# Attention and feed-forward in one pass: unread products on PE, mask products moved ahead, one query tile transposed on PE

## The chip, the cores and the metric

The kernel runs on one core of a Trainium2 chip. The metric is the device time of one execution in microseconds (us). The core has five engines that run side by side and wait for each other by semaphores: PE (matrix products; loading its weights is shown apart as PEld), DVE and ACT (elementwise work; ACT has the exponentials and the gelu), POOL (elementwise work on SBUF, and here the queue that issues all loads) and SP (here the queue that issues stores and DMA transposes).

## The reference

Eight batches of eight heads, 576 positions, head width 64. A query sees the keys within 32 positions of it. The result, heads side by side, is the input of a feed-forward layer with 512 inputs and 2048 hidden units.

```python
scores = (q @ k.T) / 8                      # per batch and head
scores = where(|i - j| <= 32, scores, -1e9)
attn   = softmax(scores)
x      = (attn @ v)  ->  4608 tokens x 512
h      = x @ w_in                           # 512 x 2048
g      = h * sigmoid(1.702 * h)
out    = g @ w_out                          # 2048 x 512
```

## The kernel before

All 8 x 576 positions are treated as one line of 4608 tokens. A **unit** u is 128 of them (36 units), a **window** w is two units, and a **tile** i is 512 tokens of queries or keys (9 tiles). Everything is in bf16, sums are in f32 in PSUM. The order of all instructions is written out by hand; nothing is moved by a scheduler. Each engine works through its own list in that order, so an instruction that waits holds up all that stand behind it on its engine.

The steps of one unit:

- `load_heads` and `load_v` (POOL queue) load queries and keys of a tile, and V of a unit (`ve`). `odd_v` copies V shifted by 64 tokens into `vo`.
- `keys_T` and `queries_T` turn a tile: PE transposes against the identity into a PSUM bank `tp`, and a copy (line 99) brings it into the rings `kT` and `qT`, for one pair of heads at a time. A faster form first lets DVE pair up the heads (`pair_heads`, into `kc` and `qc`), so that four transposes of 128 x 128 do a pair instead of eight. From tile 3 on, queries are not turned on PE: `queries_X` issues one DMA transpose of the whole tile on the SP queue. `queries_wrap` copies the first columns of the query ring behind its end, on DVE, when a tile lands at the ring's start (tiles 0, 3 and 6).
- `scores` (line 221): 32 or 64 small products into two banks of kind "a", then the exponential on ACT into `p` (line 227).
- `band` (lines 242 and 247): DVE multiplies `p` by a 0/1 mask, two products of 128 x 512 for a unit. The last unit, 35, has another layout and takes four products of 128 x 256, on line 247.
- `values` (line 258): PE multiplies `p` by `ve` and `vo`; a column of ones gives the softmax sum. `norm` (lines 269 and 270): DVE takes the reciprocal and scales into `x`.
- `x_T`: `x` is turned, in the opening on PE and with a copy, later by a DMA transpose on the SP queue.
- `layer1` (line 297): eight products of 128 x 256 and one gelu on ACT (line 299) make one of eight groups for two units. `layer2` (line 308): sixteen products of 128 x 512 in four quarters; then DVE copies the bank `o_ps` to `o_sb` (line 312) and SP stores it.

PSUM has eight banks, handed out by kind: two "h" (layer 1, and layer 2 of odd units), one "o" (layer 2 of even units), one "t" (transposes), four "a" (scores, values, some transposes).

Two layers lie between attention and output: window w runs attention for units 2w and 2w+1, layer 1 for window w-1 and layer 2 for window w-2. `head` is the opening: it prepares the masks, loads, turns tiles 0, 1 and 2, and runs the attention of units 0 to 6 with the first layers in between. In batch 0 the tokens 512 to 575 end a batch in the middle of a unit, and so queries and keys of these 64 tokens are loaded and turned apart (`load_edge`, `edge_T`). `window` runs windows 4 to 19; window 4 has an order of its own. At its end `feed` prepares what the next window needs: the shifted V, the paired heads, and in odd windows the query transpose of a tile.

Three places in it matter for the change. In window 4, the four key blocks of tile 3 alternate with groups of layer 1, and `queries_X(3)` is issued ahead of them (lines 504 to 513). In windows 5 to 14, which have two key blocks each, DVE's list has a key copy, the o_sb copy, the first mask products, the other key copy, and the second mask products. In the opening, the edge of the keys is turned and copied between the scores of units 0 and 1 and their mask products (lines 364 to 369), and its load stands behind three loads of V (lines 331 to 335).

Of the kernel before, what the change touches and what calls it, by code (L numbers as in the profile page):

```python
# [15 lines left out]
F32 = mybir.dt.float32  # L16
BF16 = mybir.dt.bfloat16
# [4 lines left out]
JT = 4  # L22
# [5 lines left out]
class _Kernel:  # L28
# [35 lines left out]
    def setup(self):  # L64
        nc, cst = self.nc, self.cst
        self.ident = cst.tile([128, 128], BF16, name="ident")
        self.mask = cst.tile([128, 4, SQ], BF16, name="mask")
        self.w_in_sb = cst.tile([128, self.NK, self.DFF], BF16, name="w_in_sb")
        self.w_out_sb = cst.tile([128, self.NFF, self.DM], BF16, name="w_out_sb")
        self.kT = cst.tile([128, 4, RING + 64], BF16, name="kT")  # L70
        self.qT = cst.tile([128, 4 * JT, RP + 16], BF16, name="qT")
        self.k_first = cst.tile([128, 4, 64], BF16, name="k_first")
        self.q_first = cst.tile([128, 4 * JT, 8], BF16, name="q_first")
        self.ve = [cst.tile([128, self.H, 66], BF16, name=f"ve{i}") for i in range(NV)]
        self.vo = [cst.tile([128, self.H, 66], BF16, name=f"vo{i}") for i in range(NV)]
        self.v_first = cst.tile([64, self.H, 66], BF16, name="v_first")
        make_identity(nc, self.ident)
        for i in range(NV):
            nc.vector.memset(self.ve[i][:, :, self.D:], 1.0)
# [63 lines left out]

    def heads_T(self, c, i, hp, kind):

        tp = self.bank(kind, [128, JT, 128], BF16, "tp")
        for j in range(JT):
            for t in range(2):
                self.nc.tensor.transpose(tp[64 * t:64 * t + 64, j, :],  # L149
                                         self.stage[c, i][:, 2 * hp + t, j * self.D:(j + 1) * self.D], self.ident)  # L150
        return tp

    def keys_T(self, i, hp, kind="t", eng=None):

        if ("k", i, "c") in self.stage:
            tp = self.bank(kind, [128, JT, 128], BF16, "tp")
            for j in range(JT):
                self.nc.tensor.transpose(tp[:, j, :], self.stage["k", i, "c"][:, hp, j], self.ident)  # L158
        else:
            tp = self.heads_T("k", i, hp, kind)  # L160
        at = (512 * i) % RING

        def put(dst, n):
            self.cast(eng or self.nc.vector, dst.rearrange("r (p j) -> r p j", j=JT),
                      tp[:, :, :n // JT].rearrange("r j p -> r p j"))

        put(self.kT[:, hp, at:at + 512], 512)
        if at == 0 and i:
            put(self.kT[:, hp, RING:], 64)
# [131 lines left out]
    def layer2(self, u, quarter, kind="o"):  # L301
# [8 lines left out]
        if quarter == 3:  # L310
# [7 lines left out]
            else:  # L318
                n = self.N - row
                nc.sync.dma_start(self.out[row:row + n, :], o_sb[:n])  # L320
                nc.sync.dma_start(self.out[0:128 - n, :], o_sb[n:])


    def head(self):

        nc, dve, act, pool = self.nc, self.nc.vector, self.nc.scalar, self.nc.gpsimd
        self.setup()
        for h in (0, 4):
            for c in "kq":
                self.load_heads(0, c, (h, h + 4))  # L330
        for m in range(3):
            self.load_v(m)
        self.setup_mask()
        for c in "kq":
            self.load_edge(c)
        self.load_v(3)
        self.load_v(4, 0)
        self.load_w_in(0)
        self.load_w_in(1)
# [16 lines left out]
        for c in "kq":  # L356
            self.load_heads(2, c)
        kinds = "htho"
        for half in (0, 2):
            for hp in (half, half + 1):  # L360
                self.keys_T(0, hp, kinds[hp], dve)
            for hp in (half, half + 1):
                self.queries_T(0, hp, kinds[hp ^ 2], act)
        self.scores(0)
        self.scores(1)
        self.edge_T("k", "h", dve)
        self.edge_T("q", "h", act)
        self.band(0)
        self.band(1)
        self.scores(2)  # L370
        self.values(0, "hh")
        self.norm(0)
# [25 lines left out]
        l2 = [(lambda c=c, u=u: self.layer2(u, c, "hhot"[u])) for c in range(4) for u in range(4)]  # L398
# [25 lines left out]
        run(1)  # L424
        self.x_T(4, "a")
        run(1)
        self.x_T(5, "a")
        self.load_v(8)
        self.load_v(9)
        self.load_v(10)  # L430
# [27 lines left out]
    def window(self, w):  # L458
# [9 lines left out]
        def run(lst, n=1):  # L468
            for _ in range(min(n, len(lst))):
                lst.pop(0)()  # L470
# [9 lines left out]
        if w == 4:  # L480
# [23 lines left out]
            for c in "qk":  # L504
                for hp in range(4):
                    self.pair_heads(c, 3, hp, dve)
                if c == "q":
                    self.queries_X(3)
            run(l1, 3)
            for _ in range(3):  # L510
                run(kt)
                run(l1)
            run(kt)
            self.feed(w)
            return
        loads()
# [2 lines left out]
            if w > 5:  # L519
                self.scores(b)  # L520
        run(l2, 2)
        run(kt)
        run(l2)
        if w == 5:
            self.scores(b)
        run(l2)
        if att:
            self.band(a)
        run(kt)
        run(l2)  # L530
        if att:
            self.band(b)
        run(l2)
        if att:
            self.values(a)
            self.values(b)
            self.norm(a)
            self.x_T(a)
            self.norm(b)
            self.x_T(b)  # L540
        run(l2, 2)
        run(l1, 4)
        self.feed(w)
# [73 lines left out]
```

## Time and profile before

| what | value |
|---|---|
| median of 3 runs | 341.6 us (340.18 to 343.05) |
| the profiled execution | 341.15 us |
| its span, from the first to the last instruction | 339.5 us |
| what lies around the span | 1.65 us |
| mean granted clock of PE | 0.99 |
| PE busy | 304.7 us, 90% of the span |
| ACT, DVE and POOL busy | 174.1, 146.6 and 73.0 us |

A row of the timeline gives the start, the duration, the engine, the line and the operation with its tiles, how many were merged into the row (x16), and in brackets how long the engine was idle before it and what ended the wait. L297 is line 297 of the kernel. A row that merges several instructions begins with the first and covers them all. In the view of stretches each engine has its busy time and number of instructions, then come the clock, a DMA share and GB/s. PE's products overlap in a pipeline, so their rows overlap too, and the distance from one start to the next tells the pace. A few records of products are missing, which leaves small gaps such as 0.16 us "issue" in front of a row with x7 instead of x8.

### The profile page before, as it was taken

Reading aid. Unit: us, or ns where it says so; the run is one execution under the profiler, and the core shown is the slowest. Engines: PE = TensorE matmul, PEld = TensorE weight load, DVE = VectorE, ACT = ScalarE, POOL = GpSimd, SP = SyncE. Lnnn points to the kernel's source line nnn. Section 1 sums busy time; section 2 is a strip of 40 time slices with the busy share of each in tenths; the row PEclk is TensorE's granted clock in tenths of the full one; section 3 lists DMA queues with packets and bytes.
Section 4 is the critical chain, followed back from the end, with each engine's and each line's share of the span. In section 5 each row is a group of like instructions: output and inputs, shape, how many; then the busy total and the mean of one; then the engine's idle time right before and its main releaser. Section 6 shows DMA issues by size and latency. Waiting matters only on the chain.

```text
span 339.5 us, 8719 instructions
## 1 busy us (share of the span) xinstructions
PE 304.7 (90%) x3748; PEld 207.4 (61%) x3784; DVE 146.6 (43%) x433; ACT 174.1 (51%) x263; POOL 73.0 (22%) x107
## 2 busy tenths in 40 slices
PE   1789999899919979999999999999999999989994
PEld 1558754656605748575757576766666675748571
DVE  1362057458507262727182818181816153442101
ACT  1555554482603727474737383838382837474150
POOL 8993464306003120322040202020200000000000
PEclk9999999999978999999999999999999999999999
DMA  7999999948984999399959989671953040302011
GB/s 89 171 199 193 186 193 190 185 84 100 149 87 58 144 118 119 55 157 128 99 65 155 147 74 80 110 87 41 93 95 75 22 86 14 90 20 75 28 35 62
DMA packets 94429, 35.29 MB, mean 104 GB/s; under 512 B 67256, under 2 KB 89784, under 8 KB 94392
## 3 DMA queue, kind: packets, MB, share of 16 engines
q0 software_dynamic: 61760, 18.49, 60.5%
q1 hardware_dynamic: 32632, 16.26, 29.3%
q8 instruction: 29, 0.48, 0.6%
q14 instruction: 8, 0.07, 0.1%
HBM read 36.96 MB, written 9.44 MB: 137 GB/s over the span
## 4 chain that ended last, share of the span: by engine, by line
PE 74%; DVE 12%; DMA 7%; issue 3%; POOL 2%; ACT 1%; POOLq 0%; ACTq 0%
PE h_ps L297 37%; PE o_ps L308 30%; DMA qT<-qc 5%; DVE p L242 4%; DVE o_sb L312 3%; PE sc L221 3%; PE pv L258 3%; DMA edge<-in_k_dram 2%; DVE kT L99 2%; PE tp L149 1%; DVE x L270 1%; PE tp L158 1%; POOL ve L133 1%; DVE p L247 1%; ACT p L227 1%
## 5 line engine op out<-in xcount | busy, mean ns | idle before, releaser
L299 ACT ACTIVATE g<-h_ps 128x512 bf16<-128x512 f32 x144 | 86.0, 597 | 123.8 <-PE h_ps L297 123.8
L297 PE MATMUL h_ps<-xT,w_in_sb 128*128 128x256 bf16 x1152 | 133.4, 275 | 2.8 <-DVE xT L99 2.1
L308 PE MATMUL o_ps<-w_out_sb,g 128*128 128x512 bf16 x540 | 129.0, 381 | 6.8 <-issue 6.3
L297 PEld LDWEIGHTS <-w_in_sb 128*128 128x128 bf16 x1152 | 112.4, 98 | 21.5 <-issue 2.5
L308 PEld LDWEIGHTS <-g 128*128 128x128 bf16 x576 | 52.5, 98 | 57.5 <-issue 2.9
L133 POOL DMA_DIRECT2D ve<-in_v_dram x40 | 33.8, 851 | 161.3 <-PE pv L258 98.1
L99 DVE COPY kT<-tp 128x512 bf16<-128x512 bf16 (+2 forms) x45 | 26.0, 596 | 97.8 <-PE tp L158 65.8
L312 DVE COPY o_sb<-o_ps 128x512 f32<-128x512 f32 x36 | 24.9, 691 | 68.6 <-PE o_ps L308 67.0
L227 ACT ACTIVATE p<-sc 128x512 bf16<-128x512 f32 x70 | 36.4, 602 | 12.8 <-PE sc L221 12.7
L270 DVE TENSOR_TENSOR x<-pv,rec 128x256 bf16<-128x256 f32 x72 | 30.6, 425 | 2.5
L242 DVE TENSOR_TENSOR p<-p,mask 128x512 bf16<-128x512 bf16 x70 | 27.1, 428 | 1.5 <-ACT p L227 1.1
L221 PE MATMUL sc<-qT,kT 64*64 64x64 bf16 x1152 | 15.3, 200 | 7.6 <-DVE qT L189 7.1
L258 PEld LDWEIGHTS <-p 128*64 128x64 bf16 x576 | 13.7, 115 | 13.8 <-DVE p L242 8.5
L299 ACT ACT_TABLE_LOAD x16 | 20.5, 1283 | 0.3
L258 PE MATMUL pv<-ve,p 128*64 128x65 bf16 x288 | 18.7, 203 | 1.9 <-DVE p L242 0.4
L221 PEld LDWEIGHTS <-kT 64*64 64x64 bf16 x1152 | 12.7, 113 | 12.4 <-issue 12.0
L227 ACT ACT_TABLE_LOAD x15 | 19.2, 1283 | 0.3
L258 PE MATMUL pv<-vo,p 128*64 128x65 bf16 x288 | 18.6, 203 | 0.7 <-DVE p L247 0.6
L99 ACT COPY qT<-tp 128x512 bf16<-128x512 bf16 (+1 forms) x13 | 7.2, 571 | 15.8 <-PE tp L149 15.5
L269 DVE RECIPROCAL rec<-pv 128x4 f32<-128x4 f32 x72 | 12.5, 174 | 6.2 <-PE pv L258 6.2
L127 POOL DMA_DIRECT2D qs<-in_q_dram x17 | 12.3, 731 | 3.4 <-DMA w_out_sb<-in_moe_w_out_dram 1.8
L127 POOL DMA_DIRECT2D ks<-in_k_dram x17 | 12.2, 723 | 2.0 <-DMA qs<-in_q_dram 1.2
(42 smaller groups left out, 100.4 us busy)
## 6 DMA issues: line engine op xcount, KB each, us to landing
out_dram<-o_sb SPq DMA_DIRECT2D x70, 128.0 KB
ve<-in_v_dram POOLq DMA_DIRECT2D x32, 128.0 KB, 7.7
w_in_sb<-in_moe_w_in_dram POOLq DMA_DIRECT2D x4, 512.0 KB, 7.6
w_out_sb<-in_moe_w_out_dram POOLq DMA_DIRECT2D x4, 512.0 KB, 10.6
ks<-in_k_dram POOLq DMA_DIRECT2D x4, 256.0 KB, 8.4
qs<-in_q_dram POOLq DMA_DIRECT2D x4, 256.0 KB, 12.0
ks<-in_k_dram POOLq DMA_DIRECT2D x2, 448.0 KB, 10.7
qs<-in_q_dram POOLq DMA_DIRECT2D x2, 448.0 KB, 14.1
```

Source lines behind the costliest of these rows:

```text
L99: (eng.copy if eng is self.nc.scalar else eng.tensor_copy)(out, in_)
L127: self.nc.gpsimd.dma_start(self.stage[key][off // JT:(off + m) // JT, lo:hi, :], src[b, lo:hi, s:s + m, :].rearrange("h (p j) d -> p h (j ...
L133: self.nc.gpsimd.dma_start(self.ve[m % NV][off:off + n, :, :self.D], self.v[b, :, s:s + n, :].rearrange("h s d -> s h d"))
L221: nc.tensor.matmul(sc[eo][lo:lo + 64, 2 * hp + blk, :], self.kT[r, hp, at:at + 64], self.qT[r, JT * hp:JT * hp + JT, q0:q0 + 16], start=(n ...
L227: nc.scalar.activation(p[:, eo], sc[eo], AF.Exp, scale=self.scale)
L242: self.nc.vector.tensor_mul(pv, pv, msk.to_broadcast([128, 4, 2, SQ]))
L258: nc.tensor.matmul(acc[half][blk * 64:blk * 64 + 64, hh, :], p[:, h % 2, h // 2 * 2 + blk, :], vt[:, h, :D + 1], start=(hh == 0), stop=(hh ...
L270: nc.vector.tensor_mul(x[:, hs, :], acc[half][:, :, :D], rec[:, hs, :].to_broadcast([128, 4, D]))
L297: nc.tensor.matmul(hps[:, i, :], self.w_in_sb[:, kr, ff * 128:(ff + 1) * 128], self.xT[t][:, kr, :], start=(i == 0 and kr == 0), stop=(i = ...
L299: nc.scalar.activation(self.g[t][:, 2 * d:2 * d + 2, :], hps, AF.Gelu_apprx_sigmoid)
L308: nc.tensor.matmul(o_ps, self.g[t][:, ff, s * 128:(s + 1) * 128], self.w_out_sb[:, ff, :], start=(ff == 0), stop=(ff == self.NFF - 1))
L312: nc.vector.tensor_copy(o_sb, o_ps)
```

## The change

Five edits, all in the order of the work or in who does it; the result stays the same.

1. `keep_busy(n)` issues n products of a cleared operand (128 x 128 by 128 x 256) into a bank of kind "a" that nobody reads. In the opening there are 24 ahead of the first key transposes, then 10, 6, 4 and 1 between the transposes of keys and queries: 45 in all. DVE clears the operand `idle` first of all.
2. The edge queries and keys are loaded ahead of V and of the mask's preparation; and the mask products of units 0 and 1 stand ahead of the edge's transposes and copies.
3. The copy of unit 5's `x` goes from DVE to ACT.
4. In window 4 the queries of tile 3 are turned on PE from the paired heads (`heads_T` now has that form too), one pair behind each pair of keys, with the copy on ACT. The DMA transpose of tile 3 is gone; those of later tiles stay.
5. In the later windows both units' mask products follow the first key copy directly. The second key block goes behind the values and norms. In window 5 the second scores go ahead of the first key block.

```diff
+        self.idle = cst.tile([128, 256], BF16, name="idle")
+        nc.vector.memset(self.idle, 0.0)
...
     def heads_T(self, c, i, hp, kind):
         tp = self.bank(kind, [128, JT, 128], BF16, "tp")
         for j in range(JT):
+            if (c, i, "c") in self.stage:
+                self.nc.tensor.transpose(tp[:, j, :], self.stage[c, i, "c"][:, hp, j], self.ident)
+                continue
             for t in range(2):
...
     def keys_T(self, i, hp, kind="t", eng=None):
-        if ("k", i, "c") in self.stage:
-            tp = self.bank(kind, [128, JT, 128], BF16, "tp")
-            for j in range(JT):
-                self.nc.tensor.transpose(tp[:, j, :], self.stage["k", i, "c"][:, hp, j], self.ident)
-        else:
-            tp = self.heads_T("k", i, hp, kind)
+        tp = self.heads_T("k", i, hp, kind)
...
+    def keep_busy(self, n):
+        junk = self.bank("a", [128, 256], F32, "junk")
+        for _ in range(n):
+            self.nc.tensor.matmul(junk, self.idle[:, 0:128], self.idle, start=True, stop=True)
...
     def head(self):
...
-        for m in range(3):
-            self.load_v(m)
-        self.setup_mask()
         for c in "kq":
             self.load_edge(c)
-        self.load_v(3)
+        self.setup_mask()
+        for m in range(4):
+            self.load_v(m)
...
+        self.keep_busy(24)
         for half in (0, 2):
             for hp in (half, half + 1):
                 self.keys_T(0, hp, kinds[hp], dve)
+            self.keep_busy(4 if half else 10)
             for hp in (half, half + 1):
                 self.queries_T(0, hp, kinds[hp ^ 2], act)
+            self.keep_busy(1 if half else 6)
         self.scores(0)
         self.scores(1)
+        self.band(0)
+        self.band(1)
         self.edge_T("k", "h", dve)
         self.edge_T("q", "h", act)
-        self.band(0)
-        self.band(1)
...
-        self.x_T(5, "a")
+        self.x_T(5, "a", act)
...
     def window(self, w):
...
                     self.pair_heads(c, 3, hp, dve)
-                if c == "q":
-                    self.queries_X(3)
-            run(l1, 3)
-            for _ in range(3):
+            run(l1, 2)
+            for hp in range(4):
                 run(kt)
+                self.queries_T(3, hp, "a", nc.scalar)
                 run(l1)
-            run(kt)
             self.feed(w)
             return
...
         run(l2, 2)
-        run(kt)
-        run(l2)
         if w == 5:
             self.scores(b)
+        run(kt)
         run(l2)
         if att:
             self.band(a)
-        run(kt)
-        run(l2)
-        if att:
             self.band(b)
         run(l2)
+        run(l2, 2)
         if att:
             self.values(a)
...
             self.x_T(b)
+        run(kt)
         run(l2, 2)
```

In the opening, DVE's list changes behind the key copies of tile 0 (the copies are line 99 before and line 101 after; `pv` is the values' bank). Before:

```order
L99 COPY kT<-tp 128x512 x4
L99 COPY kT<-tp 128x4x64
L242 TENSOR_TENSOR p<-p,mask 128x512 x4
L269 RECIPROCAL rec<-pv_366 128x4
L270 TENSOR_TENSOR x<-pv_366,rec 128x256
```

and after the change:

```order
L101 COPY kT<-tp 128x512 x4
L242 TENSOR_TENSOR p<-p,mask 128x512 x4
L101 COPY kT<-tp 128x4x64
L269 RECIPROCAL rec<-pv_418 128x4
L270 TENSOR_TENSOR x<-pv_418,rec 128x256
```

The four mask products of units 0 and 1 have moved ahead of the edge copy (128x4x64).

In window 6, DVE's list from its first key copy to the copy behind the norms is before:

```order
L99 COPY kT_70<-tp_2004 128x512
L312 COPY o_sb_2018<-o_ps_1995 128x512
L242 TENSOR_TENSOR p_1955<-p_1955,mask_67 128x512 x2
L99 COPY kT_70<-tp_2024 128x512
L242 TENSOR_TENSOR p_1992<-p_1992,mask_67 128x512 x2
L269 RECIPROCAL rec_2078<-pv0_2041 128x4
...
L312 COPY o_sb_2100<-o_ps_2030 128x512
```

and after the change:

```order
L101 COPY kT_70<-tp_2079 128x512
L242 TENSOR_TENSOR p_2030<-p_2030,mask_67 128x512 x2
L242 TENSOR_TENSOR p_2067<-p_2067,mask_67 128x512 x2
L312 COPY o_sb_2097<-o_ps_2070 128x512
...
L270 TENSOR_TENSOR x_2154<-pv1_2129,rec_2155 128x256
L101 COPY kT_70<-tp_2161 128x512
L312 COPY o_sb_2175<-o_ps_2101 128x512
```

Both pairs of mask products now stand ahead of the first o_sb copy, and the second key copy stands between the last norm and the second o_sb copy.

In window 4, PE's list around the last key block of tile 3 and the scores of unit 10 (`h_ps` is layer 1's bank, `kc` and `qc` the paired heads; each row of weights and product comes four or eight times) is before:

```order
L297 MATMUL h_ps_1610<-xT_1106,w_in_sb_68 128x256
L158 LDWEIGHTS kc_1534
L158 MATMUL tp_1620<-ident_66,kc_1534 128x128
...
L221 LDWEIGHTS kT_70
L221 MATMUL sc0_1637<-qT_71,kT_70 64x64
```

and after the change:

```order
L152 LDWEIGHTS kc_1585
L152 MATMUL tp_1679<-ident_66,kc_1585 128x128
...
L152 LDWEIGHTS qc_1580
L152 MATMUL tp_1686<-ident_66,qc_1580 128x128
...
L297 LDWEIGHTS w_in_sb_68
L297 MATMUL h_ps_1692<-xT_1158,w_in_sb_68 128x256
...
L221 MATMUL sc0_1712<-qT_71,kT_70 64x64
```

Four transposes of queries follow each four of keys, and a group of layer 1 now stands between the last transposes and the scores.

## The prediction

> **What bounds the kernel now.** I read the page's totals first.
>
> ```profile
> span 339.5 us, 8719 instructions
> PE 304.7 (90%) x3748; PEld 207.4 (61%) x3784; DVE 146.6 (43%) x433; ACT 174.1 (51%) x263; POOL 73.0 (22%) x107
> ```
>
> PE sets the end. Its work can hardly shrink, so what can be won is time in which PE stands still, or runs slowly: 339.5 - 304.7 = 34.8 us idle. To see where, I cut the span at the scores that open each window, with the view of stretches (the first row is window 5, then 6, 7, 9 and 15; the column after the stretch is its length, then PE busy).
>
> ```profile
> 90.61:115.92 25.31, 17.61 (x199) 11.54 (x200) 11.13 (x35) 9.18 (x14) 4.62 (x6) 0.87 1.05 83
> 115.92:133.82 17.90, 15.76 (x199) 10.86 (x200) 7.66 (x22) 9.41 (x14) 1.76 (x2) 1.00 1.74 139
> 133.82:150.29 16.47, 15.98 (x199) 11.04 (x200) 8.64 (x26) 9.41 (x14) 5.06 (x7) 1.00 0.91 90
> 166.76:183.36 16.60, 15.98 (x200) 11.04 (x201) 8.86 (x28) 9.41 (x14) 3.50 (x4) 1.00 0.80 84
> 265.82:281.47 15.65, 15.33 (x191) 10.51 (x193) 5.99 (x18) 9.41 (x14) 0.00 (x0) 1.00 0.24 52
> ```
>
> Windows 5 to 14 issue the same work, yet window 5 takes 9 us longer, at a mean clock of 0.87. The timeline says why:
>
> ```profile
> 84.98 9.61 SPq L184 DMA_TRANSPOSE qT<-qc  x1
> 101.31 0.20 DVE L189 COPY qT<-qT 128x128 bf16<-128x128 bf16 x1 [8.11 <-DMA qT<-qc]
> 101.56 0.59 PE L221 MATMUL sc<-qT,kT 64*64 64x64 bf16 x28 [7.09 <-DVE qT L189]
> ```
>
> The DMA transpose of tile 3's queries starts at 84.98 and is only done 16.3 us later. DVE's wrap copy waits for it, the scores of unit 11 wait for the copy, and PE idles 7.1 us.
>
> **Tile 3 queries on PE: -9.1.** Added are 16 transposes on PE and 4 copies on ACT; one DMA transpose and its packets go. The host is a loop like this one:
>
> ```profile
> 88.97 0.40 PE L158 MATMUL tp<-ident,kc 128*128 128x128 bf16 x4
> 89.20 1.04 PE L297 MATMUL h_ps<-xT,w_in_sb 128*128 128x256 bf16 x8
> 89.41 0.82 DVE L99 COPY kT<-tp 128x512 bf16<-128x512 bf16 x2 [0.49 <-PE tp L158]
> 90.28 0.23 PEld L158 LDWEIGHTS <-kc 128*128 128x128 bf16 x4 [0.32 <-DVE kT L99]
> L99 ACT COPY qT<-tp 128x512 bf16<-128x512 bf16 (+1 forms) x13 | 7.2, 571 | 15.8 <-PE tp L149 15.5
> L299 ACT ACTIVATE g<-h_ps 128x512 bf16<-128x512 f32 x144 | 86.0, 597 | 123.8 <-PE h_ps L297 123.8
> ```
>
> Rounds start every 1.31 us (88.97, 90.28), because the one bank of kind "t" is free only when DVE has copied it (89.41 + 0.82). PE issues 0.23 + 0.87 in a round, so 0.2 is spare, and four more transposes (0.23) just fill it. ACT's round is one gelu and one copy, 0.60 + 0.57, under 1.31. The last round gains a group of layer 1 that stood earlier before, so in all I count +0.1. The wrap copy then stands behind 6 DVE copies (about 2 us after the last key copy), while PE has a layer-1 group, scores and 8 products of layer 2 to issue (about 3 us): hidden, and if that cover failed, some tenths. A window with keys and no stall is window 15 plus two key blocks, 15.65 + 2 x 0.22 = 16.1. So 25.3 - 16.1 = 9.2, less 0.1. That includes about 1.3 of slow clock behind the gap. Bounds: 7.1 (the idle row alone) and 9.5.
>
> **Mask products straight behind the exps: -4.0.** Window 8 shows the order that the change rewrites (the last two rows are window 15):
>
> ```profile
> 152.31 2.07 ACT L227 ACTIVATE p<-sc 128x512 bf16<-128x512 f32 x4
> 154.85 0.69 DVE L312 COPY o_sb<-o_ps 128x512 f32<-128x512 f32 x1 [1.03 <-PE o_ps L308]
> 156.12 0.69 DVE L99 COPY kT<-tp 128x512 bf16<-128x512 bf16 x1
> 156.72 0.75 DVE L242 TENSOR_TENSOR p<-p,mask 128x512 bf16<-128x512 bf16 x2
> 156.69 0.22 PE L258 MATMUL pv<-ve,p 128*64 128x65 bf16 x1
> 158.10 1.67 PE L308 MATMUL o_ps<-w_out_sb,g 128*128 128x512 bf16 x7 [0.16 <-issue]
> 271.78 0.22 PE L258 MATMUL pv<-ve,p 128*64 128x65 bf16 x1
> 272.81 1.67 PE L308 MATMUL o_ps<-w_out_sb,g 128*128 128x512 bf16 x7 [0.16 <-issue]
> ```
>
> Between the exps, done at 154.38, and the second pair of mask products, done at 157.47, DVE copies an o_ps and a key tile; PE reached the values at 156.69, and their block lasts 158.10 - 156.69 = 1.41. In window 15, without key copies, it lasts 1.03, and in window 6, where PE came late, 0.87 (124.30 to 125.17). So six windows lose 0.54, the two of 16.60 another 0.13 each, windows 15 and 16 lose 0.16: 6 x 0.54 + 2 x 0.67 + 0.3 = 4.9. Behind the change both pairs (0.75 each) end near 155.2 and nothing waits. What is late next: the second key copy now stands between the norms and the copy of o_ps, whose bank the second layer-1 group needs. By the rows' durations the norms end 2.6 after the values begin, the key copy at 3.3, the o_sb copy at 4.0, and PE wants the bank at 3.9: about 0.1 in 9 windows, 0.9 in all. Bounds: 1.5 and 4.9.
>
> **Window 6 and the last values: -2.0.** Two more rows, and the exps and products of unit 35:
>
> ```profile
> 122.92 1.46 PE L308 MATMUL o_ps<-w_out_sb,g 128*128 128x512 bf16 x6 [1.82 <-issue]
> 300.11 2.44 ACT L229 ACTIVATE p<-sc 128x512 bf16<-128x512 f32 x2
> 302.73 2.08 DVE L247 TENSOR_TENSOR p<-p,mask 128x256 bf16<-128x256 bf16 x4
> ```
>
> The 1.82 in window 6 has no semaphore behind it, and falls inside a group of products. Nothing in the change removes it; a stall tied to the instruction stream's place may move or go. I take half, -0.9 (bounds 0 and -1.8). For unit 35 the last of four products (0.52 each) ends at 304.8; behind the second exp (302.55) its two remaining products would end at 303.6: -1.1 (bounds -0.5 and -1.2).
>
> **Unit 5's copy on ACT: -0.8.**
>
> ```profile
> 59.99 0.41 DVE L99 COPY xT<-tp 128x512 bf16<-128x512 bf16 x1
> 60.45 0.81 PE L297 MATMUL h_ps<-xT,w_in_sb 128*128 128x256 bf16 x6 [1.57 <-DVE xT L99]
> ```
>
> Layer 1 waits for the last copy of its input, which stands behind an o_sb copy on DVE. ACT is idle then and takes about 0.59; PE starts near 59.6, when unit 4's copy on DVE is done too. Bounds 0.4 and 0.9.
>
> **The opening: -2.2.** Here three edits meet: 45 unread products (24, 10, 6, 4, 1), edges ahead of V, and products ahead of the edge copy.
>
> ```profile
> 4.59 2.67 POOL L133 DMA_DIRECT2D ve<-in_v_dram  x3
> 15.00:20.00 5.00, 4.36 (x110) 3.19 (x110) 4.17 (x13) 3.78 (x8) 4.72 (x8) 1.00 1.33 201
> 5.63 1.07 PE L149 MATMUL tp<-ident,ks 128*64 128x128 bf16 x16 [5.63 <-DMA ks<-in_k_dram]
> 11.71 1.06 PE L149 MATMUL tp<-ident,qs 128*64 128x128 bf16 x16 [0.36 <-DVE kT L99]
> 13.58 0.69 POOL L140 COPY vo<-ve 64x528 bf16<-64x528 bf16 x1
> 13.88 2.06 ACT L227 ACTIVATE p<-sc 128x512 bf16<-128x512 f32 x4 [0.41 <-PE sc L221]
> 15.69 0.29 DVE L99 COPY kT<-tp 128x256 bf16<-128x256 bf16 x1 [3.43 <-PE tp L202]
> 15.90 2.12 DVE L242 TENSOR_TENSOR p<-p,mask 128x512 bf16<-128x512 bf16 x4
> 21.34 1.86 PE L297 MATMUL h_ps<-xT,w_in_sb 128*128 128x256 bf16 x8 [0.67 <-ACT xT L99]
> 26.12 1.05 PE L297 MATMUL h_ps<-xT,w_in_sb 128*128 128x256 bf16 x8
> ```
>
> Eight products of 256 columns take 1.86 at 21.34 and 1.05 at 26.12: 213 ns apart against 109, so PE runs at half speed until about 26, whatever the clock row shows. The turn came 4 to 5 us after layer 1 began. The 24 products at half speed are 24 x 0.213 = 5.1 us, from about 1.1, when DVE has cleared their operand; so I expect the full clock from about the first key transposes.
>
> [...]
>
> The four loads still pace the transposes: the last begin at 11.7 and end some 0.5 sooner, and scores and exps follow 0.5 sooner. The products no longer wait for the edge copy (3.43 idle on DVE); they follow the exps and end near 15.9, not 18.0. Next in line is V: its loads are issued 3.3 later (two edge loads and the mask), so POOL's vo copies start near 14.7, not 13.58, and the first values come at 16.3, not 16.73. So layer 1 starts near 19.9 instead of 21.34 (-1.4); its first two groups save up to 0.8 each if the clock has held through the sparse stretch ahead of them. Chained to the norms that makes -2.8 if held, -1.7 if not: I take -2.2. Cost if the clock never rises: 45 x 0.213 = 9.6 us do not fit the 8.5 of idle that PE has before 11.71 (11.71 less three blocks of 1.07), the last transposes end 1.7 late, and the term is about 0. Bounds 0 and -3.5. POOL's issue of later weights slips by about 1 us, into a load stream that is full until then.
>
> **The sum** against the profiled execution (341.15, of which 339.5 span): 9.1 + 4.0 + 2.0 + 0.8 + 2.2 = 18.1, giving 323.05, say 323.0. The median of the three runs, 341.6, lies 0.45 above, within their spread of 340.18 to 343.05.
>
> **Rivals.**
> 1. The clock is not released by these products, or falls again before layer 1: the opening gives 0, 325.2. For: from 15 to 20 us PE was busy for 4.36 of 5 with small products, and still slow at 21.34. Against: 5.1 us unbroken. [...]
> 2. The o_sb copy becomes the wait of each window with keys: if the whole key copy (0.69) lands on the path in 9 windows, 6.2 replaces 0.9: 328.3. For: the margin is 0.1. Against: kind "h" has two banks.
> 3. Slower than before: the DMA transposes that remain become late. Tile 4's is issued 21.3 us before window 7's scores,
>
> ```profile
> 112.49 10.30 SPq L184 DMA_TRANSPOSE qT<-qc  x1
> ```
>
>   and with the 16.3 us of tile 3 that leaves 5; window 6 without its stall leaves 3, and tiles 5 and 6 have about as much. If three of them took 26 us, each would cost 7 idle and 1.3 of slow clock: 323 + 25 = 348. It decides from about 25 us each, where the 18 won are gone; against it, no window from 7 on shows such a wait today.
>
> **Chances.** The forecast 0.67, rival 1 0.17, rival 2 0.11, rival 3 0.05, of which 0.02 reach beyond +1% and 0.03 only eat up the gain. About 1% is what a measurement of this kernel tells from no change. So faster 0.95, same 0.03, slower 0.02. Range: all terms at their good end give 341.15 - 22 = 319, at their bad end 331; with the spread of runs, and leaving out the corners, 318.5 to 329.5, which holds rivals 1 and 2.
>
> **What would show it.** No DMA transpose near 85 and no PE gap behind unit 11's first scores; window 5 about 16 us at full clock; values blocks of 0.9 in windows 7 to 14; layer 1's first eight products near 1.05 and starting near 20; its long stretch starting near 26.5 instead of 29.0. Wrong if window 5 still holds an idle of several us, if layer 1 shows a gap of 0.5 or more at its second group, or if the first groups of layer 1 still take 1.86.

## The result, and the profile after

The changed kernel takes 326.92 us (median of 4 executions, 326.33 to 327.22) where the kernel before takes 341.89 (340.18 to 343.05): a ratio of 0.956, 95% interval 0.952 to 0.961, or 15.0 us less. The profiled execution took 326.33, with a span of 324.6, so against the one of before (341.15) the traces have 14.8 us to account for, where the sum had 18.1. The page's totals of the changed kernel:

```profile
span 324.6 us, 8899 instructions
PE 310.2 (96%) x3845; PEld 209.1 (64%) x3845; DVE 147.0 (45%) x433; ACT 176.3 (54%) x268; POOL 73.0 (22%) x107
```

PE's busy time has grown by 5.5 and its idle time fell from 34.8 to 14.4. Not all of that is real: the trace of before has 540 of layer 2's 576 products, this one has all, and layer 2's busy time alone went from 129.0 to 133.1. The view of stretches, cut again at the scores that open each window, shows windows 5, 6, 7, 9, 10 and 15 (behind the stretch its length, then PE busy):

```profile
88.44:104.90 16.46, 16.20 (x201) 10.86 (x200) 10.22 (x33) 9.41 (x14) 4.46 (x6) 1.00 0.98 91
104.90:121.17 16.27, 16.01 (x201) 10.88 (x200) 7.54 (x22) 9.41 (x14) 1.76 (x2) 1.00 1.74 142
121.17:137.44 16.27, 16.01 (x201) 10.86 (x200) 8.54 (x26) 9.41 (x14) 5.08 (x7) 1.00 0.93 89
153.71:170.11 16.40, 16.01 (x201) 10.89 (x200) 8.69 (x28) 9.41 (x14) 3.50 (x4) 1.00 0.95 94
170.11:186.97 16.86, 16.11 (x202) 10.96 (x201) 8.00 (x25) 9.41 (x14) 1.75 (x2) 1.00 1.88 135
252.05:267.53 15.48, 15.48 (x194) 10.43 (x194) 6.24 (x18) 9.41 (x14) 0.00 (x0) 1.00 0.23 53
```

Window 5 lost 8.85 us, window 6 lost 1.63, but the windows from 7 on only 0.2 each, where 0.4 had been forecast, and window 10 grew. The reason stands in the timeline of window 6 (the first row is the start of the values), and in the list of waits (us in total, times, longest):

```profile
111.08 0.59 PEld L258 LDWEIGHTS <-p 128*64 128x64 bf16 x32 [0.42 <-issue]
...
113.64 0.68 DVE L101 COPY kT<-tp 128x512 bf16<-128x512 bf16 x1
113.67 1.04 PE L297 MATMUL h_ps<-xT,w_in_sb 128*128 128x256 bf16 x8
114.24 0.68 DVE L312 COPY o_sb<-o_ps 128x512 f32<-128x512 f32 x1
114.97 1.25 PE L297 MATMUL h_ps<-xT,w_in_sb 128*128 128x256 bf16 x10 [0.26 <-DVE o_sb L312]
```

```profile
PE h_ps L297 <- DVE o_sb L312: 2.7, 10, 0.4
```

The first layer-1 group starts at 113.67. The next would start one group later, 8 x 0.109 = 0.87, at 114.54, but it takes the bank that the o_sb copy reads until 114.92, and that copy stands behind the second key copy. PE stands still for 0.43 (the row puts 0.26 on the copy; the ends of products are modelled). The list counts ten such waits: one in each of windows 5 to 9 and 11 to 14, and one in window 17, which has no key copy.

In window 5 the queries' transposes follow the keys' with no wait of their own; the next round starts 1.32 later:

```profile
83.07 0.39 PE L152 MATMUL tp<-ident,kc 128*128 128x128 bf16 x4
83.29 0.39 PE L152 MATMUL tp<-ident,qc 128*128 128x128 bf16 x4
83.52 1.04 PE L297 MATMUL h_ps<-xT,w_in_sb 128*128 128x256 bf16 x8
84.39 0.39 PE L152 MATMUL tp<-ident,kc 128*128 128x128 bf16 x4
```

And the opening, in the timeline of PE and then in stretches (the column after POOL is the granted clock):

```profile
1.14 5.30 PE L327 MATMUL junk<-idle 128*128 128x256 bf16 x24 [1.14 <-DVE ve L81]
7.21 1.26 PE L327 MATMUL junk<-idle 128*128 128x256 bf16 x10
20.08 1.87 PE L297 MATMUL h_ps<-xT,w_in_sb 128*128 128x256 bf16 x8 [0.67 <-ACT xT L101]
22.46 1.80 PE L297 MATMUL h_ps<-xT,w_in_sb 128*128 128x256 bf16 x8
24.61 1.05 PE L297 MATMUL h_ps<-xT,w_in_sb 128*128 128x256 bf16 x8
```

```profile
13.80:17.20 3.40, 1.62 (x85) 1.35 (x81) 3.09 (x8) 2.89 (x7) 2.77 (x5) 1.00 1.70 177
17.20:20.60 3.40, 2.58 (x47) 1.67 (x35) 2.68 (x8) 2.81 (x5) 3.18 (x6) 0.50 1.23 202
20.60:24.00 3.40, 3.40 (x31) 2.17 (x29) 1.58 (x6) 1.33 (x2) 3.27 (x9) 0.50 1.23 194
```

The first 24 products ran 0.213 apart and the ten from 7.21 on at 0.11: the clock came up near 7.0. It fell again at 17.2 and was back at 24.0, so the first two groups of layer 1 still ran at about half speed (1.87 and 1.80 for eight, against 1.05). Layer 1's long stretch starts at 27.50 instead of 29.01.

### The profile page after: what moved, and what is told of

Read it like the earlier page. It is cut to its first block, busy times and chain, and to the rows that moved or that the text cites. A ratio compares the mean times of both kernels' runs of the same rounds, so it can differ in the third digit from the quotient of the medians.

```text
span 324.6 us, 8899 instructions
## 1 busy us (share of the span) xinstructions
PE 310.2 (96%) x3845; PEld 209.1 (64%) x3845; DVE 147.0 (45%) x433; ACT 176.3 (54%) x268; POOL 73.0 (22%) x107
## 4 chain that ended last, share of the span: by engine, by line
PE 78%; DVE 12%; issue 4%; ACT 3%; DMA 2%; POOL 1%; DVEq 0%; POOLq 0%; ACTq 0%
PE h_ps L297 37%; PE o_ps L308 31%; DVE x L270 4%; PE sc L221 3%; DVE o_sb L312 3%; PE pv L258 2%; DMA qs<-in_q_dram 2%; DVE kT L101 2%; DVE rec L269 2%; PE tp L155 1%; PE tp L152 1%; ACT L227 1%; DVE p L242 1%; ACT p L227 1%; PE tp L285 1%
## 5 line engine op out<-in xcount | busy, mean ns | idle before, releaser
L308 PE MATMUL o_ps<-w_out_sb,g 128*128 128x512 bf16 x576 | 133.1, 380 | 0.0
L308 PEld LDWEIGHTS <-g 128*128 128x128 bf16 x576 | 53.2, 98 | 57.1
L258 PEld LDWEIGHTS <-p 128*64 128x64 bf16 x576 | 11.8, 113 | 11.0 <-issue 8.9
L101 ACT COPY qT<-tp 128x512 bf16<-128x512 bf16 (+1 forms) x17 | 9.6, 574 | 15.1 <-PE tp L155 15.1
L258 PE MATMUL pv<-ve,p 128*64 128x65 bf16 x288 | 14.5, 199 | 2.1 <-ACT qT L101 0.8
L221 PEld LDWEIGHTS <-kT 64*64 64x64 bf16 x1152 | 11.9, 107 | 5.8 <-issue 5.3
L221 PE MATMUL sc<-qT,kT 64*64 64x64 bf16 x1152 | 14.5, 194 | 1.0 <-ACT p L227 0.6
L258 PE MATMUL pv<-vo,p 128*64 128x65 bf16 x288 | 14.5, 199 | 0.2 <-DVE p L247 0.2
```

What stands on the lines that cost most here:

```text
L101: (eng.copy if eng is self.nc.scalar else eng.tensor_copy)(out, in_)
L221: nc.tensor.matmul(sc[eo][lo:lo + 64, 2 * hp + blk, :], self.kT[r, hp, at:at + 64], self.qT[r, JT * hp:JT * hp + JT, q0:q0 + 16], start=(n ...
L258: nc.tensor.matmul(acc[half][blk * 64:blk * 64 + 64, hh, :], p[:, h % 2, h // 2 * 2 + blk, :], vt[:, h, :D + 1], start=(hh == 0), stop=(hh ...
L308: nc.tensor.matmul(o_ps, self.g[t][:, ff, s * 128:(s + 1) * 128], self.w_out_sb[:, ff, :], start=(ff == 0), stop=(ff == self.NFF - 1))
```

## The experiments

Eleven runs follow, in three groups. Each group has its own executions of the kernel before, and the ratios go by these: their median was 341.44 beside the first four runs (without the unread products, the two on tile 3's queries, o_sb first), 340.12 beside the next four (the old order, the first run that holds the clock, the other banks, the shifted kernel), and 340.46 beside the last three. Numbers of a single window are from one profiled execution each.

### Without the unread products

```
-        self.keep_busy(24)
...
-            self.keep_busy(4 if half else 10)
...
-            self.keep_busy(1 if half else 6)
```

> The changed kernel without its 45 unread products, all else as it is. Theory A: they lift the clock only from 7.0 to 17.2 us, where PE is mostly waiting for loads, ACT and DVE, and layer 1 begins at half speed with or without them; so little is lost: the long stretch of layer 1 starts 0.3 to 1.0 us later than 27.50, and the time is 327.2 to 328.0. Theory B: the whole 1.5 us that the opening gained comes from the clock: 328.4, and the long stretch of layer 1 starts at 29.0. Theory C: the products do nothing: 326.9 within 0.2, and the gain of the opening is the order of loads and copies.

Measured: 327.87 (327.23 to 328.12), ratio 0.961, 0.959 to 0.964. The opening of this kernel, PE's timeline:

```profile
21.27 1.87 PE L297 MATMUL h_ps<-xT,w_in_sb 128*128 128x256 bf16 x8 [0.67 <-ACT xT L101]
23.64 1.89 PE L297 MATMUL h_ps<-xT,w_in_sb 128*128 128x256 bf16 x8
26.04 1.55 PE L297 MATMUL h_ps<-xT,w_in_sb 128*128 128x256 bf16 x8
29.43 0.83 PE L297 MATMUL h_ps<-xT,w_in_sb 128*128 128x256 bf16 x6 [0.52 <-DVE xT L101]
```

The long stretch starts at 29.43, 1.93 later than with the products. Four more profiles below have the changed opening as it is (the DMA back, o_sb first, the old order, the shifted kernel), and there it starts at 27.64 to 27.95. So the products are worth 1.5 to 1.9 in the opening, as theory B has it or a little more, though the time itself lies in the range of theory A. Whether the new order of loads and copies does anything by itself isn't shown: the opening of before, in the three profiles that have it (before, its second profile, and tile 3's queries on PE alone), starts this stretch at 29.01, 30.14 and 29.12, and 29.43 lies among them. Between the two profiled executions the time rose by 1.47, the 1.93 less the 0.46 by which window 10 is shorter here (16.40, without the idle time of 0.75 in the changed kernel); the medians lie 0.95 apart, since the profiled execution of the changed kernel was its shortest.

### Tile 3's queries by DMA again, and on PE alone

The first kernel is the changed one with its one DMA transpose back, the second the kernel before with the 16 transposes on PE as its only edit:

```
-            for hp in range(4):
+                if c == "q":
+                    self.queries_X(3)
+            run(l1, 3)
+            for _ in range(3):
                 run(kt)
-                self.queries_T(3, hp, "a", nc.scalar)
                 run(l1)
```

> The changed kernel with tile 3's queries again by one DMA transpose. Theory A: the transpose takes some 16 us again, the scores of unit 11 wait 7 us for it, and the clock falls in that gap: window 5 lasts about 25.3 instead of 16.46, window 4 loses its 0.24, and the time is 326.9 + 8.6 = 335.5. Theory B: since window 4 and the opening run at other times now, the transpose meets less traffic and comes in 12 us or less: window 5 lasts 21 or less and the time is at most 331.

> The kernel before with one edit: tile 3's queries transposed on PE, nothing else. Theory A: the edit alone is worth the 8.6 us that windows 4 and 5 show, so 341.9 - 8.6 = 333.3, and window 5 lasts about 16.5 to 17.0 (the mask products are still behind the copies). Theory B: only the idle row of 7.1 is won and the slow clock behind it stays: 334.8. For the 1.82 us idle without a semaphore in window 6: if it is tied to that place of the instruction stream it is there again or moved; if it was an accident of the profiled execution it is gone.

Measured: 338.2 (337.22 to 340.57; ratio 0.992, 0.989 to 0.996) with the DMA back, 332.0 (331.34 to 332.74; ratio 0.974, 0.971 to 0.978) with the edit alone. With the DMA back, timeline and stretch of window 5:

```profile
101.35 0.59 PE L221 MATMUL sc<-qT,kT 64*64 64x64 bf16 x28 [10.42 <-DVE qT L189]
```

```profile
88.50:117.47 28.97, 17.86 (x199) 11.70 (x200) 11.37 (x35) 9.18 (x14) 4.46 (x6) 0.82 1.09 74
```

PE comes to these scores 8.0 us behind the transpose's issue (82.98) instead of 9.5, and they can start 18.4 behind it instead of 16.6, so the wait grew from 7.1 to 10.4, and the slow clock behind it with it: theory A's mechanism with too small a number, 11.3 instead of 8.6. Of the 3.3 that the wait grew, 1.5 is PE coming sooner and 1.8 the transfer taking longer. The edit alone gave 9.4: window 5 went from 25.31 to 16.65, and window 6 from 17.90 to 16.47, because the 1.82 us without a semaphore is gone. In the second profile of before, shown below, window 5 lasts 26.08 and window 6 has no such stall, so there the 9.4 is in window 5 alone.

### The o_sb copy ahead of the second key copy

```
-        run(kt)
         run(l2, 2)
+        run(kt)
         run(l1, 4)
```

> The changed kernel with the second key block of each window moved behind the two layer-2 groups that follow the values, so that DVE copies o_ps ahead of the second key tile. Theory A: the 0.35 to 0.43 us that PE waits for o_sb in each of ten windows comes from that key copy standing first; it goes, windows 7 to 14 last about 15.9 instead of 16.27, and the time is 326.9 - 10 x 0.36 = 323.3. Theory B: the wait is the norms' length, not the key copy, and the order does not matter: 326.9 within 0.4. Theory C: the key block, issued later, makes layer 1 or the next block of keys wait in its turn, and half is given back: 325.1.

Measured: 324.32 (322.92 to 325.21), ratio 0.951, 0.948 to 0.953. Its stretches for windows 7, 8, 10 and 15, and a row of window 10 from its timeline:

```profile
120.97:136.82 15.85, 15.53 (x199) 10.89 (x200) 8.56 (x26) 9.41 (x14) 5.09 (x7) 1.00 0.89 94
136.82:152.68 15.86, 15.54 (x200) 10.89 (x202) 7.57 (x22) 9.41 (x14) 1.78 (x2) 1.00 2.23 136
168.53:186.42 17.89, 15.73 (x200) 10.97 (x202) 8.10 (x25) 9.41 (x14) 1.75 (x2) 1.00 2.25 134
249.83:265.31 15.48, 15.16 (x192) 10.45 (x194) 6.24 (x18) 9.41 (x14) 0.00 (x0) 1.00 0.21 53
```

```profile
177.19 0.22 PE L258 MATMUL pv<-ve,p 128*64 128x65 bf16 x1 [1.85 <-issue]
```

Theory A holds: a window falls from 16.27 to 15.85, by the whole 0.42, and nothing is given back. The total fell by 2.6 instead of 3.6, for the most part because the idle time in window 10, which no semaphore explains, grew from 0.75 to 1.85. Beside window 15, 15.48 without key blocks, a window with them now costs 0.37 more, as much as PE is busier in it (15.53 against 15.16): what is left is the work of the eight transposes.

### The old order in the windows

```
         run(l2, 2)
+        run(kt)
+        run(l2)
         if w == 5:
             self.scores(b)
-        run(kt)
         run(l2)
         if att:
             self.band(a)
+        run(kt)
+        run(l2)
+        if att:
             self.band(b)
         run(l2)
-        run(l2, 2)
...
-        run(kt)
         run(l2, 2)
```

> The changed kernel with the order of the kernel before inside the windows (key blocks and o_ps copies ahead of and between the mask products); the opening, tile 3's queries and unit 5's copy as changed. Theory A: the new order is worth 0.2 in each of eight windows, 0.17 in two, and 1.1 at unit 35, so windows 7 to 14 last 16.47 again and the time is 326.9 + 2.9 = 329.8, less the 0.6 to 0.9 of the idle time in window 10 if that does not come back. Theory B: it is worth what was forecast for it, 4.0 and 1.1: 332.0.

Measured: 330.98 (329.77 to 332.43), ratio 0.973, 0.968 to 0.977. Windows 6, 7 and 8 of its profiled execution (330.21):

```profile
105.25:121.72 16.47, 16.30 (x201) 11.05 (x201) 7.64 (x22) 9.41 (x14) 1.76 (x2) 1.00 1.68 139
121.72:139.29 17.57, 16.53 (x201) 11.15 (x201) 8.64 (x26) 9.41 (x14) 5.07 (x7) 1.00 1.05 96
139.29:155.76 16.47, 16.30 (x202) 11.03 (x201) 7.64 (x22) 9.41 (x14) 1.78 (x2) 1.00 2.01 132
```

Windows are 16.47 again, 0.2 more, as theory A has it; window 7 holds another idle stretch without a semaphore (0.87). The median lies 4.1 above the changed kernel's, between the theories; the profile bears out A window by window, and puts 1.1 of the rest on that stretch.

### Holding the clock up to layer 1

```
         self.scores(2)
+        self.keep_busy(7, "t")
-        self.values(0, "hh")
+        self.values(0, "hh", 6)
...
+        self.keep_busy(4)
         self.x_T(0, "h", act)
         self.x_T(1, "h", act)
+        self.keep_busy(6)
```

The 6 in the values stand between their two halves. The edit ran on the kernel with o_sb first, twice, and on the changed kernel.

> The kernel with o_sb copied first, and 23 more unread products in the stretch between 14.8 and 20.4 us, where PE waits: 7 behind the scores of unit 2, 6 between the halves of unit 0's values, 4 and 6 around the two transposes of x ahead of layer 1. Theory A: the clock fell at 17.2 because PE was idle most of that stretch; filled, it holds, layer 1's first two groups take 1.05 instead of 1.87 and 1.38 to 1.80, unit 1's values and scores(3) run at full speed too, and the long stretch of layer 1 starts 1.2 to 1.8 sooner: 322.8 if the 1.85 us idle in window 10 stays, 321.0 if the shift of the instruction stream by 46 moves it away. Theory B: small products and waits count for nothing, the clock falls all the same, and the fillers only delay what waits: 324.3 to 324.7, with layer 1's first group at 1.87.

> The kernel with o_sb copied first and 23 more unread products, unchanged, with more executions: its profiled execution took 320.8 but two of its four 328 to 329.5, which its profile does not explain. [...] Theory B: the long ones were a passing disturbance: the times lie within 320.5 to 323.

> The changed kernel with only the 23 more unread products in the opening, its windows as they are. Theory A: they hold the clock up to layer 1, worth the 1.0 us that the long stretch of layer 1 started sooner beside the kernel with o_sb first, and the 0.75 us idle in window 10 moves with the shift of 46 instructions: 325.2 to 326.0, all executions within 1.5 us. Theory B: what makes the long executions is in the fillers themselves (they shift the loads or the opening): then here too some executions take 5 us more.

Measured: 325.15 over four executions (320.81 to 329.54; ratio 0.945, 0.940 to 0.950, without the two longest) and 323.15 over six more (322.09 to 324.35; ratio 0.949, 0.946 to 0.952) on the kernel with o_sb first. On the changed kernel, 326.26 over four of six executions (324.56 to 326.65; ratio 0.958, 0.955 to 0.962); the other two, 333.6 and 333.8, lie apart and are left out. The opening in the first of these runs, stretches and timeline:

```profile
13.80:17.20 3.40, 2.79 (x67) 2.10 (x63) 3.05 (x7) 2.93 (x7) 3.23 (x5) 1.00 1.55 177
17.20:20.60 3.40, 3.12 (x77) 2.50 (x77) 3.06 (x9) 2.60 (x5) 3.18 (x6) 1.00 1.21 194
```

```profile
20.29 1.03 PE L299 MATMUL h_ps<-xT,w_in_sb 128*128 128x256 bf16 x8
21.64 1.05 PE L299 MATMUL h_ps<-xT,w_in_sb 128*128 128x256 bf16 x8
26.76 3.45 PE L299 MATMUL h_ps<-xT,w_in_sb 128*128 128x256 bf16 x30 [0.52 <-DVE xT L101]
```

With PE busy for 2.79 of the 3.40 us from 13.8 instead of 1.62, the clock reads 1.00 to 20.6 instead of 0.50 from 17.2, layer 1's first two groups take 1.03 and 1.05, and the long stretch starts at 26.76. In the other two runs it starts at 26.88 and 26.02, against 27.50 to 27.95 in the five profiles of the opening without these fillers. The time is another matter. The six further executions on the kernel with o_sb first have a ratio of 0.949 against 0.951 without the edit, intervals overlapping, and on the changed kernel 0.958 against 0.956; and two executions of 328.0 and 329.5, and two of 333.6 and 333.8, stand against none more than 3.4 above the shortest of its kernel in the 30 of the kernels above. Every profile here is of a shorter one, so what the long ones wait for stays open.

### Other banks for the first values

```
-        self.values(0, "hh")
+        self.values(0, "ot")
...
-        self.values(1, "ot")
+        self.values(1, "hh")
...
-        self.x_T(0, "h", act)
-        self.x_T(1, "h", act)
+        self.x_T(0, "o", act)
+        self.x_T(1, "t", act)
```

> The kernel with o_sb copied first, and in the opening unit 0's values in the banks of kinds o and t and unit 1's in the two of kind h, instead of the other way round. Theory A: unit 0's values wait for banks that the edge copies hold (0.80 on ACT, 0.72 on DVE); in free banks they start when the mask products of unit 0 and V's shifted copy are done, near 15.2, and end near 16.0 instead of 17.03; unit 1's then wait for POOL's second shifted copy (done 16.89), so the chain gains 0.5 to 0.8: 323.5 to 323.8. Theory B: V's shifted copies on POOL are what paces, and unit 1's values gain nothing: 324.3.

Measured: 324.17 (323.23 to 326.05), ratio 0.953, 0.949 to 0.958, against 0.951 without the swap. From the first scores to the first layer-1 group it is 8.24 us in both profiles (12.61 to 20.85, and 12.15 to 20.39): theory B, the banks were not what the chain waited for last.

This profiled execution, at 326.05 the longest of its four, shows what a stall can cost. Window 10 holds one of 1.94, the products behind it run slower (seven of layer 2 take 2.85 us from 177.61, and 1.67 in the changed kernel, from 174.68), and the window lasts 19.66 instead of 15.85:

```profile
177.43 0.19 PE L258 MATMUL pv<-ve,p 128*64 128x65 bf16 x1 [1.94 <-issue]
```

### The idle time without a semaphore

Two kernels were for this. The first has the first 24 products of 256 columns as 48 of 128; the second is the kernel before, unchanged.

```
-        self.keep_busy(24)
+        self.keep_busy(48, 128)
```

> The kernel with o_sb copied first, with the first 24 unread products of 256 columns as 48 of 128: the same work and time, but 48 more instructions in PE's stream ahead of everything. [...] Theory B: the stall belongs to what is done at that place (the values of unit 20), whatever the count of instructions: window 10 lasts 17.9 again, 324.3.

> The kernel before, unchanged, profiled a second time. If the 1.82 us idle without a semaphore in window 6 depends on when a block of PE's instructions is fetched in that execution, it is gone or of another length, and window 6 lasts 16.1 to 17.9; if it is tied to the place of the instruction stream alone, it is there again at 1.8, and the same group of layer-2 products is cut.

Measured: 325.48 (323.96 to 326.47; ratio 0.955, 0.951 to 0.960) and one execution of 341.66. Windows 6, 7, 10 and 11 of the shifted kernel, and its idle rows:

```profile
104.94:122.02 17.08, 16.03 (x202) 10.83 (x202) 7.66 (x22) 9.41 (x14) 1.76 (x2) 1.00 1.60 133
122.02:138.71 16.69, 16.02 (x202) 10.95 (x202) 8.57 (x26) 9.41 (x14) 5.10 (x7) 1.00 0.84 87
170.41:186.26 15.85, 15.85 (x201) 10.87 (x200) 8.02 (x25) 9.41 (x14) 1.75 (x2) 1.00 1.86 136
186.26:204.19 17.93, 16.06 (x202) 11.02 (x201) 8.38 (x26) 9.41 (x14) 2.25 (x3) 1.00 0.70 90
```

```profile
114.70 0.40 PE L152 MATMUL tp<-ident,kc 128*128 128x128 bf16 x4 [1.05 <-issue]
123.36 0.22 PE L221 MATMUL sc<-qT,kT 64*64 64x64 bf16 x4 [0.67 <-issue]
188.77 0.30 PE L221 MATMUL sc<-qT,kT 64*64 64x64 bf16 x8 [1.87 <-issue]
```

Window 10, which lasted 17.89, is 15.85: what is done there does not make the stall. Three others turned up, in windows 6, 7 and 11, so nothing was won. In the kernel before, profiled again, window 6 is 16.47 and the 1.82 is gone, though not an instruction is different. (The time is no shorter for it: the opening and window 5 took 1.1 and 0.8 longer in that execution.)

```profile
117.83:134.30 16.47, 15.98 (x199) 11.03 (x200) 7.64 (x22) 9.41 (x14) 1.76 (x2) 1.00 1.48 141
```

No row names what this idle time waits for. The DMA queues show something beside it. The page of the changed kernel counts 30 packets and 0.49 MB, so 16 KB each, on the queue that it calls `instruction`, and a stretch of 5 us holds one (columns: packets, MB, share of 16 engines), first the one ahead of its stall (172 to 177), then one from later (188 to 193), in a fence each:

```profile
q8 instruction: 1, 0.02, 5.0%
```

```profile
q8 instruction: 1, 0.02, 1.1%
```

5.0% of 16 engines for 5 us is 4.0 us for 16 KB (from 172.33 to 176.32 in the records), 1.1% is 0.9. The 0.75 us idle in window 10 ends at 177.68, 1.36 behind the end of that packet. With o_sb first, whose 1.85 us idle end at 177.19, the packet in the stretch from 171 to 176 has 5.3%, so 4.2 us.

That PE waited for such a packet in these two is an estimate of mine, from these times alone. Two things fit a wait that has to do with PE's list of instructions: the place moves when 24 products are added ahead of everything (the shifted kernel), and the same program has the idle time in one execution and not in the next (the kernel before). Two others do not bear the estimate out. Another packet of the changed kernel, from 149.08 to 153.08, took 4.0 us as well, and no idle time of PE without a semaphore follows it. And in the kernel before the last packet ahead of the 1.82 took 1.12 and ended at 118.60, 4.3 ahead of the end of that idle time (122.92). So no run shows what these two wait for, nor what the others do: the 1.82 of before, the 1.05, 0.67 and 1.87 of the shifted kernel, the 1.94 of the swapped banks, the 0.87 of the old window order, and one of 0.67 in the second run that holds the clock.

## Why the prediction was right, and where it was not

The forecast of 323.0 with a range of 318.5 to 329.5 met 326.9: the direction and the largest term were right, and the sum was 3.3 too large. Step by step, from the two profiled executions:

- **Tile 3's queries, -9.1.** Windows 4 and 5 gave 8.85 - 0.24 = 8.6. Rounds of 1.32 were as worked out, and window 5 is 16.46 rather than 16.1 + 0.1 only because the o_sb wait stands in it. The step was right, and the bounds (7.1 and 9.5) held it.
- **Mask products, -4.0: the step that failed.** The gain was worked out as 4.9 less an o_sb wait of "about 0.1 in 9 windows, 0.9 in all". Windows 7 to 16 gave 1.5 (1.9 without the idle time in window 10). The gain itself was there and somewhat larger: with the o_sb copy first, a window takes 15.85 against 16.47, 0.62 each. What was mis-sized is the wait: about 0.42 in ten places, and not 0.1 in nine. Counted from the start of the values (111.08), the o_sb copy ends at 3.84, where I had 4.0; but PE wants the bank at 3.46, where I had 3.9. My values block was too long: I had taken 1.03 or 0.87 from rows of before, where it is 0.63 in the changed kernel (111.08 to 111.71, where the key transposes follow). The rows behind it show why:

```profile
111.71 0.40 PE L152 MATMUL tp<-ident,kc 128*128 128x128 bf16 x4
111.95 1.89 PE L308 MATMUL o_ps<-w_out_sb,g 128*128 128x512 bf16 x8
```

  Eight products stand where before had seven and 0.16 "issue": the first one's record was missing there, and its 0.22 had gone into the length of the block. With 0.63 for the block, 0.24 for four transposes, 1.72 for eight products and 0.87 for a layer-1 group, PE wants the bank at 3.46. With a margin of 0.1 an error of 0.4 decides. Rival 2 named this mechanism and priced it at 0.69; it came at six tenths of that.
- **Window 6, -0.9.** It gave 1.63, and window 10 lost 0.46 to a stall of the same kind. By the second profile of before, this was never the change's doing: it comes and goes between executions. So the term came out by luck.
- **Unit 35, -1.1**: from the scores of window 17 to the layer-1 group behind unit 35's values, 9.83 became 8.72, as forecast. The tail behind it took 0.4 more, which was not in the sum: it is the o_sb wait once more, here behind the norms of unit 35 without a key copy (the group before started at 291.72, so this one could have at 292.59):

```profile
293.02 1.14 PE L297 MATMUL h_ps<-xT,w_in_sb 128*128 128x256 bf16 x9 [0.27 <-DVE o_sb L312]
```

- **Unit 5's copy, -0.8**: from the start of layer 1's long stretch to the layer-1 group that reads unit 5's `x`, 31.44 became 30.55, so 0.9.
- **The opening, -2.2**: 1.5. I had put it between a clock that holds (-2.8) and one that does not (-1.7), and it did not. Against the experiment without the products, the products are worth 1.5 to 1.9, and the order of loads and copies nothing that these profiles show: without the products the first group of layer 1 starts at 21.27, where before had 21.34. So the 1.3 by which this group starts sooner in the changed kernel (20.08) came from the clock that the products raised, and not, as I had it with -1.4, from mask products that no longer wait. (A slip besides, on which nothing hung: 9.6 of unread products against 8.5 of idle make 1.1 late, not 1.7.) The -2.8 rested on a clock that lasts through the sparse stretch ahead of layer 1, and no run shows that without more products there: the changed kernel's fell at 17.2, behind 3.40 us in which PE was busy for 1.62.

Rival 1, the clock falling again before layer 1, came true in its condition but not in its price (the opening kept 1.5 instead of 0). With it came one of the three signs that I had named for being wrong: the first groups of layer 1 still took 1.87 and 1.80. A second one, a gap of 0.5 or more at layer 1's second group, was missed by little, at 0.43. Rival 3 did not show in a profile of the changed kernel: tile 4's transpose took 13.5 us from its issue to its last packet, and that was 6 ahead of the scores that read it.

The best kernel that the study is sure of is the changed one with o_sb copied first: 324.32, ratio 0.951, 2.6 below the change. Holding the clock as well gave 323.15 in six executions, not told apart from it, and two long ones in four others.

## What to carry to other kernels

When a copy is moved out from in front of one consumer, work out to the tenth who stands behind its new place, and take the time at which the next consumer wants its bank from a window that has no wait in it: a margin of 0.1 us is no margin when the durations come from rows in which a record may be missing. Products that only keep PE busy moved the long run of real ones 1.5 to 1.9 us forward here, although the clock fell again in a stretch of small products and short waits between them (PE busy for 1.62 of 3.40 us); filling that stretch too moved it by about 1 more, and whether the time shows it stayed open. And a stall in one profile that no semaphore explains should be looked for in a second profile before a change is credited or charged with it.

## What the runs showed of the hardware

- The clock row did not always tell the pace. In the kernel without unread products it reads 1.00 while layer 1's products run at about half pace (1.87 us for eight at 21.27, against 1.04 at 27.65); in the changed kernel the same pace (1.87 at 20.08) reads 0.50.
- In the changed kernel the pace rose 5.8 us behind the first of 24 unbroken products (1.14 to 7.0), the clock fell at 17.2 and was back at 24.0. With the swapped banks the same 24 products took 4.12 us instead of 5.30, so there the pace rose sooner.
- Ahead of the fall at 17.2 PE had been busy for 1.62 of 3.40 us (from 13.80); with 2.79 in the same stretch (the first run that holds the clock) the row stays at 1.00. In the gap of 10.42 us with the DMA back it reads 0.90 from 92 to 96 and 0.50 from 96 to 101. With 1.85 us idle in window 10 (o_sb first) the window's mean clock is 1.00; with 1.94 (swapped banks) the layer-2 products behind it were slower, seven in 2.85 us instead of 1.67.
- The changed kernel's page counts 30 packets of 16 KB on the queue that it calls `instruction`; 28 of them took 0.9 to 1.4 us, two 4.0. An idle time of PE without a semaphore (0.75) ends 1.36 us behind one of these two; none follows the other. What the stalls of 0.67 to 1.94 us wait for is not shown.
- DMA transposes of the same size, one tile of queries, took from the issue to the last packet 14.4 us for tile 3 (before), 13.5 for tile 4 and 5.6 in window 11 (changed kernel). In the kernel before, the copy that waited for tile 3 started another 1.9 later, 16.3 behind the issue.
